# Moving the weight splits, the last pair's sums and copies, and small buffers in a fused attention and mixture-of-experts kernel

## The chip, the cores and the metric

One core of a Trainium2 chip runs the whole program. The metric is the time of one execution in device microseconds; "before" was run three times. TensorE is called PE in the profile, VectorE DVE, ScalarE ACT, GpSimd POOL and SyncE SP.

## The reference

Soft-capped attention of 4 batches, 12 heads, 448 positions and 64 channels; its output, 1792 tokens of 768 channels, goes through a mixture of 8 experts with one expert per token.

```python
scores = cap * tanh(q @ k.T / sqrt(64) / cap)
attn = softmax(scores)                       # exp, divided by the sum over keys
x = (attn @ v)                               # as [1792, 768]
logits = normalize(x) @ normalize(expert_emb).T / tau
e = argmax(logits); gate = softmax(logits)[e]
out[token] = gate * (relu(x[token] @ w1[e]) @ w2[e])     # w1: 768 x 1024, w2: 1024 x 768
```

## The kernel before

The attention works on pairs of heads, 24 in all, six to a batch. The loop of `attention_bounded` runs over i = 0 to 24, and in each i over four parts u = 0 to 3: PE makes part u of the scores of pair i and ACT turns them into probabilities (tanh at line 780, exp at line 784); at the same time PE multiplies the probabilities of the pair before, j = i - 1, with the values, part u (line 811, and line 820 in part 3). So i = 24 has only the values of pair 23. At part 2 DVE splits q and k of the next pair into a high and a low half (lines 756 and 757). After part 3, DVE copies the values of pair j out of PSUM (line 826; the PSUM tile "v" has one buffer), and `add_keys(i)` sums the seven tiles of probabilities over keys: first two and two on DVE (line 792), the rest on POOL (lines 794 and 800). For the last pair, where nothing comes after, half of the rest is on DVE (lines 798 and 800).

The order on each engine is the order in which the program is written down (a manual schedule). Four lists are worked off between the parts: `later` (what follows a pair: `norms` at line 837 sums over keys on PE and copies to `ds` at line 839; `rows` transposes the values on PE and scales them on DVE at line 866; `router` and more), `route` and `side` (the choice of experts for a batch), and `fill`.

`fill` holds the work on the first expert: once two batches have gone through, the expert with most tokens so far is taken first, and its weights are loaded in 14 pieces into a ring of three buffers. Each piece is split in two halves, 28 splits in all: ACT rounds a half to float16 (line 221) and DVE takes the rest (line 222), and after the second half SP loads the piece three further on (lines 691 and 694). One is taken from `fill` at a time, unless `hold` has entries, three after each of two steps of a batch's norms:

```python
if fill and u != 2 and not hold:
    fill.pop(0)()
```

Behind the loop, the first tile of the first expert begins: `transpose_x` (PE transposes at line 212, ACT and DVE copy at lines 215 and 216), then twelve steps `up(0, 0)` to `up(1, 5)` on PE (line 231), in each of which one entry of `later` and one of `fill` are taken, and a `relu` (lines 243 and 244) after each six. Then, in `tile0`, come the second half of the tile, and between its matmuls the choice of experts for the last batch. The branch that ends the attention (line 1122) leads to the second tile of the first expert. There DVE computes the order of the experts and the slots of all tokens (`order` and `slots`, lines 1174 to 1216), PE and DVE a table from it (lines 1227 and 1228), and POOL gathers the next tile's tokens with it. Tiles of the seven other experts follow, each expert's weights split while the tile before is computed.

Pools: `small` is open for the whole program; `apool` and `lpool` hold the attention's buffers; `work` is opened behind the attention and shares their memory.

Of the kernel before, what the change touches and what calls it, by code (L numbers as in the profile page):

```python
# [30 lines left out]
F32 = mybir.dt.float32  # L31
F32R = mybir.dt.float32r
F16 = mybir.dt.float16
I32 = mybir.dt.int32
AF = mybir.ActivationFunctionType
ALU = mybir.AluOpType
# [3 lines left out]
P = 128  # L40
B, H, S, DH = 4, 12, 448, 64
# [3 lines left out]
E = 8  # L45
# [3 lines left out]
G = 4 * B  # L49
# [31 lines left out]
def attention_moe(ctx: ExitStack, tc: tile.TileContext, q, k, v, cap, emb, tau, w1, w2, qk_pairs, v_pairs, out):  # L81
    nc = tc.nc
# [99 lines left out]
    sums = const.tile([P, NF], F32, name="sums")  # L182
# [85 lines left out]
    small = ctx.enter_context(tc.tile_pool(name="small", bufs=1))  # L268
    ps_t = ctx.enter_context(tc.tile_pool(name="ps_t", bufs=2, space=PSUM))
    with ExitStack() as actx:  # L270
# [71 lines left out]
        t = small.tile([P, 4, XW], F32, tag="xsb", name="xsb")  # L342
# [398 lines left out]
        def attention_bounded(apool, ps_s, ps_o):  # L741
# [18 lines left out]
            prob = {}  # L760
# [25 lines left out]
            psum_v = {}  # L786
            sums = {}

            def add_keys(i):
                pt = prob[i]  # L790
                t = apool.tile([P, 2, S], F32, tag="sums", name=f"sums{i}", bufs=3)
                nc.vector.tensor_tensor(t, pt[:, 0:2, :], pt[:, 2:4, :], op=ALU.add)  # L792
                if i < NPAIRS - 1:
                    nc.gpsimd.tensor_tensor(t, t, pt[:, 4:6, :], op=ALU.add)  # L794
                for s in range(2):
                    eng = nc.vector if i == NPAIRS - 1 and s == 0 else nc.gpsimd
                    if i == NPAIRS - 1:
                        eng.tensor_tensor(t[:, s, :], t[:, s, :], pt[:, 4 + s, :], op=ALU.add)
                    sl = slice(s * DH, (s + 1) * DH)
                    eng.tensor_tensor(t[sl, s, :], t[sl, s, :], pt[sl, 6, :], op=ALU.add)  # L800
                sums[i] = t

            def values(i, u):
                vb = loaded[i // 2][1][:, i % 2]
                pt = prob[i]
                if u == 0:
                    psum_v[i] = ps_o.tile([P, 512], F32, tag="v", name=f"v{i}")
                o = psum_v[i]
                if u < 3:
                    for s in range(2):  # L810
                        nc.tensor.matmul(  # L811
                            o[s * DH : (s + 1) * DH, :S],
                            vb[:, u, s * DH : (s + 1) * DH],
                            pt[:, 2 * u + s, :],
                            start=u == 0,
                            stop=False,
                            skip_group_check=True,
                        )
                else:
                    nc.tensor.matmul(  # L820
                        o[:, :S], vb[:, 3, :], pt[:, 6, :], start=False, stop=True, skip_group_check=True
                    )

                if u == 3:
                    x = apool.tile([P, S], F32, tag="xt", name=f"xt{i}", bufs=8)
                    nc.vector.tensor_copy(x, o[:, :S])  # L826
                    xt[i] = x

            xt = {}
# [2 lines left out]
            def norms(i):  # L832

                b, n = i // NP, i % NP
                d = ps_o.tile([P, 512], F32, tag="d", name=f"d{i}")
                for m in range(4):
                    nc.tensor.matmul(d[m * 32 : (m + 1) * 32, :S], ones32, sums[i + m // 2][:, m % 2, :], start=True, stop=True)
                ds = apool.tile([P, S], F32, tag="ds", name=f"ds{i}", bufs=1)
                nc.vector.tensor_copy(ds, d[:, :S])
                return ds  # L840

            def norms_t(i, ds):
# [59 lines left out]
            NPAIRS = B * NP  # L902
# [56 lines left out]
            with tc.manual_schedule():  # L959
                split_qk(0)  # L960
                for i in range(NPAIRS + 1):
                    j = i - 1
                    if i == 0:
                        route.extend(x for f in prepare for x in (f, lambda: None))
                    for u in range(4):
                        if i < NPAIRS:
                            scores(i, u)
                        if (i, u) == (0, 0):
                            split_qk(1)
                        if (i, u) == (0, 1):  # L970
                            warm_up()
                        if u == 2 and 0 < i < NPAIRS - 1:
                            split_qk(i + 1)
                        if j >= 0:
                            values(j, u)
                        if u != 2:
                            do_later()
                        if side:
                            side.pop(0)()
                        if u % 2 == 0 or i >= 3 * NP:  # L980
                            do_route()
                        if u == 1 and len(later) > 2:
                            do_later()
                        if fill and u != 2 and not hold:
                            fill.pop(0)()
                        if hold:
                            hold.pop()
                    if i % 2 == 0 and i // 2 + 2 < NH:
                        load_heads(i // 2 + 2)
                    if i < NPAIRS:  # L990
                        add_keys(i)
                    if j >= 0:
                        after(j)
                while route:
                    do_route()
                transpose_x(ps_t, "tt")
                scale_x()
                hp = [ps_s.tile([P, 2, 4, P], F32, tag="s", name=f"hp{h}")[:, 0] for h in range(2)]
                ups = [(h, j) for h in range(2) for j in range(DC)]
                while later or ups:  # L1000
                    do_later()
                    if ups:
                        h, j = ups.pop(0)
                        up(w1p[0], h, j, hp[h])
                        if j == DC - 1:
                            relu(h, hp[h], acc0, tiles=first_h[h])
                    if fill:
                        fill.pop(0)()
                yp = ps_s.tile([P, 2, 512], F32, tag="s", name="yp")
                tile0(fill, (lambda n, i: yp[:, i, :384] if n == "y" else x_tile, (ps_t, "tt")))  # L1010
# [133 lines left out]
    val = work.tile([P, NV, E], F32, tag="val", name="val")  # L1144
    by_pos = work.tile([P, NV, E], F32, tag="by_pos", name="by_pos")
    pos_i = work.tile([1, 2, E], I32, name="pos_i")
    pos_e = work.tile([1, E], I32, name="pos_e")
    perm = work.tile([P, E, E], F32, name="perm")
    table = work.tile([P, NTAB], I32, name="table")
    cp = {}  # L1150
    eid = {}
# [20 lines left out]
    def order():  # L1172

        nc.vector.tensor_tensor(
            perm,
            iota_t[:, :E].unsqueeze(2).to_broadcast([P, E, E]),
            place.unsqueeze(1).to_broadcast([P, E, E]),
            op=ALU.is_equal,
        )
        which = work.tile([1, E, E], F32, tag="which_e", name="which_e")  # L1180
        nc.vector.tensor_tensor(which, perm[0:1], iota_t[0:1, :E].unsqueeze(1).to_broadcast([1, E, E]), op=ALU.mult)
        with nc.allow_low_precision("numbers of experts, exact"):
            nc.vector.tensor_reduce(pos_e, which, axis=AX.X, op=ALU.add)

    def slots():
        every = work.tile([P, E], F32, tag="every", name="every")
        nc.vector.tensor_tensor(every, done_full, halves, op=ALU.add)
        gn = work.tile([P, E, E], F32, tag="gn", name="gn")
        nc.vector.tensor_tensor(gn, gt, every.unsqueeze(1).to_broadcast([P, E, E]), op=ALU.mult)
        first_t = work.tile([P, E], F32, tag="first_t", name="first_t")  # L1190
        nc.vector.tensor_reduce(first_t, gn, axis=AX.X, op=ALU.add)
        token_rows(last)

        both = work.tile([P, E], F32, tag="both", name="both")
        more = work.tile([P, E], F32, tag="more", name="more")
        nc.vector.scalar_tensor_tensor(out=both, in0=done_full, scalar=-31.0, in1=tails, op0=ALU.add, op1=ALU.mult)
        nc.vector.tensor_tensor(more, first_t, done_full, op=ALU.add)
        nc.vector.tensor_tensor(more, place, more, op=ALU.subtract)
        nc.vector.scalar_tensor_tensor(out=both, in0=both, scalar=32.0, in1=first_t, op0=ALU.mult, op1=ALU.add)
        nc.vector.scalar_tensor_tensor(out=more, in0=more, scalar=float(TAIL0), in1=tails, op0=ALU.add, op1=ALU.mult)  # L1200
        nc.vector.scalar_tensor_tensor(out=both, in0=more, scalar=1024.0, in1=both, op0=ALU.mult, op1=ALU.add)
        at = work.tile([P, G, E], F32, tag="at", name="at")
        nc.vector.tensor_tensor(at, oh_all, both.unsqueeze(1).to_broadcast([P, G, E]), op=ALU.mult)
        slot = work.tile([P, G], F32, tag="slot", name="slot")
        nc.vector.tensor_reduce(slot, at, axis=AX.X, op=ALU.add)
        packed, which, more = [work.tile([P, G], I32, tag=n, name=n) for n in ("packed", "which", "further")]
        nc.vector.tensor_scalar(packed, slot, 31.0 * 32, None, op0=ALU.add)
        nc.vector.tensor_scalar(which, packed, 5, 31, op0=ALU.logical_shift_right, op1=ALU.bitwise_and)
        nc.vector.tensor_scalar(more, packed, 10, None, op0=ALU.logical_shift_right)
# [453 lines left out]
```

## Time and profile before

| | us |
|---|---|
| runs | 547.07, 541.33, 545.64 |
| median | 545.64 |
| profiled execution | 543.0 |
| its span, first to last instruction | 541.3 |
| PE busy | 479.0 |
| DVE busy | 335.4 |
| ACT busy | 299.7 |
| POOL busy | 239.2 |

The profile is of one execution, with times from the start of its span. A row of the time line has the start, the duration, engine, line, operation, what it writes and reads, and in brackets how long the engine stood idle before it and what it stood for. Scores of pair 0 begin at 8 us, the values of pair 23 at 227 us, and the expert tiles take the rest.

### The profile page before, as it was taken

The page shows a single profiled execution, that of the slowest core. Times are in us where ns is not written, and L with a number is a line of the kernel's source. Part 1 is how long each engine was busy: PE and PEld are TensorE (multiplying, and loading weights), DVE is VectorE, ACT ScalarE, POOL GpSimd, SP SyncE. Part 2 cuts the span into 40 slices and gives each one's busy share as a digit, 9 for nine tenths or more (in the row PEclk, how much of TensorE's full clock was granted, in tenths as well). Part 3 has the DMA queues.
Part 4 walks back from the last instruction along what each step waited for, and adds up shares of the span by engine and source line. Part 5 has one row for each costly group of instructions (what it writes and reads, how often), then busy time and mean ns, then how long its engine had stood idle before and what let it go on. Part 6 is the DMA issues. An engine that isn't in the chain of part 4 may idle for free. (4 is left out here: it accounts for less than half of the span.)

```text
span 541.3 us, 11929 instructions
## 1 busy us (share of the span) xinstructions
PE 479.0 (88%) x4597; PEld 311.6 (58%) x4598; DVE 335.4 (62%) x713; ACT 299.7 (55%) x369; POOL 239.2 (44%) x289
## 2 busy tenths in 40 slices
PE   3999998999897988969879699999999999998970
PEld 1444443344433333337658488778887888787760
DVE  4877686968698899587738812591213921396811
ACT  3988788788877987917108301651114811386500
POOL 2567554655553355550125623562333643355321
PEclk9999999999999999979999799999999999999977
DMA  7433219321633540325189911293110952097940
GB/s 224 133 111 114 64 49 312 115 68 45 215 139 130 191 160 0 89 72 178 36 320 401 356 64 59 100 365 115 61 59 32 350 200 72 31 320 256 383 140 11
DMA packets 30514, 83.09 MB, mean 153 GB/s; under 512 B 7277, under 2 KB 7433, under 8 KB 30418
## 3 DMA queue, kind: packets, MB, share of 16 engines
q1 hardware_dynamic: 26354, 67.68, 35.9%
q0 software_dynamic: 2816, 12.61, 6.9%
q10 hardware_dynamic: 1248, 1.64, 0.9%
q8 instruction: 45, 0.74, 0.6%
q14 instruction: 51, 0.42, 0.2%
HBM read 69.51 MB, written 13.00 MB: 152 GB/s over the span
## 5 line engine op out<-in xcount | busy, mean ns | idle before, releaser
L780 ACT ACTIVATE prob<-s,icap 128x896 f32<-128x896 f32 x96 | 86.2, 903 | 25.8 <-PE s L774 18.2
L231 PEld LDWEIGHTS <-h 128*128 128x128 f16 x1056 | 81.5, 100 | 10.3 <-issue 6.6
L794 POOL TENSOR_TENSOR sums<-sums,prob 128x896 f32<-128x896 f32 x23 | 48.3, 2099 | 83.1 <-DVE sums L792 67.5
L784 ACT ACTIVATE prob<-prob,cap_b 128x896 f32<-128x896 f32 (+1 forms) x64 | 81.8, 1277 | 2.1
L231 PE MATMUL h<-xh,h 128*128 128x128 f16 (+1 forms) x480 | 79.6, 220 | 3.1 <-ACT x_tile L669 1.4
L231 PE MATMUL h<-xh,l 128*128 128x128 f16 (+1 forms) x480 | 79.6, 220 | 2.8 <-issue 2.8
L231 PE MATMUL h<-xl,h 128*128 128x128 f16 (+1 forms) x480 | 79.6, 220 | 0.0
L811 PE MATMUL v<-prob,vb 128*64 128x448 f32 x288 | 70.0, 565 | 3.0 <-DVE xt L826 2.9
L800 POOL TENSOR_TENSOR sums<-sums,prob 64x448 f32<-64x448 f32 x47 | 64.3, 1368 | 3.6
L204 POOL TENSOR_TENSOR x_tile<-xg 128x768 f32<-128x768 f32 x16 | 23.5, 1467 | 82.8 <-PE xt L212 72.9
L244 DVE SCALAR_TENSOR_TENSOR hl<-h,hh 128x512 f16<-128x512 f32 (+1 forms) x20 | 13.3, 664 | 65.3 <-ACT hh L243 65.3
L231 PEld LDWEIGHTS <-l 128*128 128x128 f16 x528 | 52.9, 100 | 0.8 <-issue 0.8
L243 ACT ACTIVATE hh<-h 128x512 f16<-128x512 f32 (+1 forms) x20 | 11.5, 574 | 70.1 <-PE h L231 70.1
L215 ACT CAST xh<-xt 128x384 f16<-128x384 f32 x30 | 13.1, 480 | 65.3 <-PE xt L212 57.3
L774 PE MATMUL s<-hi 64*128 64x448 f32 x144 | 34.8, 475 | 15.3 <-DVE hi L756 12.8
L1396 PE MATMUL h<-xh,h 128*128 128x160 f16 x192 | 39.9, 233 | 5.2 <-ACTq L1539 2.6
L638 PEld LDWEIGHTS <-hh 128*128 128x128 f16 (+1 forms) x352 | 32.9, 100 | 19.1 <-issue 0.5
L222 DVE SCALAR_TENSOR_TENSOR l<-w1r,by_pos,h 128x1024 f16<-128x1024 f32 x30 | 37.7, 1307 | 9.5 <-ACT h L221 9.5
L216 DVE TENSOR_TENSOR xl<-xt,xh 128x384 f16<-128x384 f32 x30 | 15.4, 551 | 43.6 <-ACT xh L215 43.5
L774 PEld LDWEIGHTS s<-hi 64*128 64x128 f32 x144 | 14.1, 188 | 47.7 <-ACT prob L780 18.9
L638 PE MATMUL y<-h,hl 128*128 128x384 f16 (+1 forms) x160 | 38.2, 329 | 2.0 <-DVE hl L244 2.0
L1396 PE MATMUL h<-xh,l 128*128 128x160 f16 x192 | 39.9, 233 | 0.0
(315 smaller groups left out, 1135.5 us busy)
## 6 DMA issues: line engine op xcount, KB each, us to landing
w1r<-in_moe_w_dram SPq DMA_DIRECT2D x36, 512.0 KB, 6.1
w2r<-in_moe_w_dram SPq DMA_DIRECT2D x24, 768.0 KB, 8.1
qkb<-in_qk_pairs_dram SPq DMA_DIRECT2D x11, 960.0 KB, 5.7
vb<-in_v_pairs_dram SPq DMA_DIRECT2D x12, 512.0 KB, 6.5
x_dram<-xsb SPq DMA_DIRECT2D x4, 1152.0 KB, 6.7
ring<-in_moe_w_dram SPq DMA_DIRECT2D x6, 512.0 KB, 4.0
ring<-in_moe_w_dram SPq DMA_DIRECT2D x8, 384.0 KB, 3.1
x_dram<-xsb ACTq DMA_DIRECT2D x1, 1152.0 KB
```

The costliest lines, as they stand in the source:

```text
L204: nc.gpsimd.tensor_tensor(x_tile, xg[:, :D], xg[:, SCALE : SCALE + 1].to_broadcast([P, D]), op=ALU.mult)
L216: nc.vector.tensor_tensor(lo, t, hi, op=ALU.subtract)
L222: nc.vector.scalar_tensor_tensor(out=lo, in0=raw, scalar=scale, in1=hi, op0=ALU.mult, op1=ALU.subtract, accum_out=acc)
L231: nc.tensor.matmul(hp[:, f, :W], l[j][:, c], x[:, j, :W], start=j == 0 and f == 0 and n == 0, stop=j == DC - 1 and f == 3 and n == 2, skip ...
L638: nc.tensor.matmul(y, hidden[h][l][:, c, o : o + k], w2p[p % 2][w][f // 2][:, f % 2, m * C : (m + 1) * C], start=f == 0 and n == 0, stop=f ...
L774: nc.tensor.matmul(sp[:, s, :S], l[sl, kc], r[sl, :], start=n == 0, stop=n == 2)
L780: nc.scalar.activation(o, d, AF.Tanh, scale=icap)
L784: nc.scalar.activation(o, o, AF.Exp, scale=cap_b)
L794: nc.gpsimd.tensor_tensor(t, t, pt[:, 4:6, :], op=ALU.add)
L800: eng.tensor_tensor(t[sl, s, :], t[sl, s, :], pt[sl, 6, :], op=ALU.add)
L811: nc.tensor.matmul(o[s * DH : (s + 1) * DH, :S], vb[:, u, s * DH : (s + 1) * DH], pt[:, 2 * u + s, :], start=u == 0, stop=False, skip_grou ...
L1396: nc.tensor.matmul(o, w1p[p % 2][l][j][:, c], x[:, j, :], start=j == 0 and f == fs[0] and m == 0, stop=j == DC - 1 and f == fs[-1] and m == 2,
```

## The change

- `fill` is taken from at all four parts of a pair, and no longer while i = 24.
- The first add of the last pair's sums (two tiles and two on DVE) has its own function, `add_two`, and is written at part 2 of i = 23, behind that part's split, instead of after part 3.
- The copy of the last pair's values and of the last sums over keys (`ds` of pairs 22 and 23) go from DVE to ACT.
- The small tiles of `order` and `slots` are taken from `small` instead of `work`.

```diff
+            def add_two(i):
+                pt = prob[i]
+                t = sums[i] = apool.tile([P, 2, S], F32, tag="sums", name=f"sums{i}", bufs=3)
+                nc.vector.tensor_tensor(t, pt[:, 0:2, :], pt[:, 2:4, :], op=ALU.add)
+
             def add_keys(i):
-                pt = prob[i]
-                t = apool.tile([P, 2, S], F32, tag="sums", name=f"sums{i}", bufs=3)
-                nc.vector.tensor_tensor(t, pt[:, 0:2, :], pt[:, 2:4, :], op=ALU.add)
+                if i < NPAIRS - 1:
+                    add_two(i)
+                pt, t = prob[i], sums[i]
...
-                sums[i] = t
...
-                    nc.vector.tensor_copy(x, o[:, :S])
+                    (nc.vector.tensor_copy if i < NPAIRS - 1 else nc.scalar.copy)(x, o[:, :S])
...
-                nc.vector.tensor_copy(ds, d[:, :S])
+                (nc.vector.tensor_copy if i < NPAIRS - 2 else nc.scalar.copy)(ds, d[:, :S])
...
-                        if fill and u != 2 and not hold:
+                        if fill and not hold and i < NPAIRS:
                             fill.pop(0)()
                         if hold:
                             hold.pop()
+                        if (i, u) == (NPAIRS - 1, 2):
+                            add_two(i)
...
-    pos_e = work.tile([1, E], I32, name="pos_e")
-    perm = work.tile([P, E, E], F32, name="perm")
+    pos_e = small.tile([1, E], I32, name="pos_e")
+    perm = small.tile([P, E, E], F32, name="perm")
...
-        every = work.tile([P, E], F32, tag="every", name="every")
+        every = small.tile([P, E], F32, tag="every", name="every")
...
```

The lines left out at the end do the same for `which_e`, `gn`, `first_t`, `both`, `more`, `at`, `slot`, `packed`, `which` and `further`.

## Rows read from the trace of the kernel before

**Rows 1.** The page of the kernel before, its parts 1 and 2.

```profile
PE 479.0 (88%) x4597; PEld 311.6 (58%) x4598; DVE 335.4 (62%) x713; ACT 299.7 (55%) x369; POOL 239.2 (44%) x289
...
PEclk9999999999999999979999799999999999999977
```

**Rows 2.** Busy time by stretch: PE, PEld, DVE, ACT, POOL, granted clock, DMA.

```profile
190.00:195.00 5.00, 4.11 (x23) 2.12 (x21) 4.90 (x11) 4.93 (x6) 4.04 (x3) 1.00 0.13 23
...
236.00:238.00 2.00, 1.21 (x7) 0.55 (x11) 2.00 (x6) 0.87 (x3) 0.42 (x2) 0.74 0.00 0
...
240.00:242.00 2.00, 2.00 (x16) 1.89 (x16) 1.48 (x4) 0.00 (x0) 0.00 (x0) 0.50 0.00 0
...
243.50:244.00 0.50, 0.50 (x4) 0.08 (x4) 0.00 (x0) 0.00 (x0) 0.00 (x0) 0.70 0.92 369
...
516.00:518.00 2.00, 0.00 (x0) 0.00 (x0) 0.00 (x0) 0.00 (x0) 0.00 (x0) 0.72 0.47 163
```

**Rows 3.** Time line of PE: start, duration, line, idle time before.

```profile
218.09 0.97 PE L811 MATMUL v<-prob,vb 128*64 128x448 f32 x4
...
227.40 0.97 PE L811 MATMUL v<-prob,vb 128*64 128x448 f32 x4 [0.28 <-DVE xt L826]
...
235.38 0.52 PE L212 MATMUL xt<-ident,x_tile 128*128 128x128 f32 x3 [3.08 <-DVE xsb L866]
...
240.00 0.27 PE L231 MATMUL hp<-xl,h 128*128 128x128 f16 x1 [0.62 <-DVE xl L216]
```

**Rows 4.** Time line of DVE at the end of the attention.

```profile
219.51 0.75 DVE L222 SCALAR_TENSOR_TENSOR l<-ring,first_s,h 128x512 f16<-128x512 f32 x1 [1.47 <-ACT h L221]
...
220.19 1.09 DVE L792 TENSOR_TENSOR sums<-prob 128x896 f32<-128x896 f32 x1
...
229.62 2.01 DVE L792 TENSOR_TENSOR sums<-prob 128x896 f32<-128x896 f32 x1
...
233.13 1.43 DVE L800 TENSOR_TENSOR sums<-sums,prob 64x448 f32<-64x448 f32 x1
...
237.64 1.83 DVE L222 SCALAR_TENSOR_TENSOR l<-ring,first_s,h 128x384 f16<-128x384 f32 x1
```

**Rows 5.** The two lines of a split: minimum/median/maximum ns.

```profile
L221 ACT ACTIVATE h<-ring,first_s x28: 597/616/718, 165.0 to 252.7; 128x384 f16<-128x384 f32 x16, 128x512 f16<-128x512 f32 x12
L222 DVE SCALAR_TENSOR_TENSOR l<-ring,first_s,h x28: 583/733/1992, 165.8 to 253.4; 128x384 f16<-128x384 f32 x16, 128x512 f16<-128x512 f32 x12
```

**Rows 6.** Time line of ACT in pairs 18 to 23.

```profile
170.09 0.23 ACT L428 ACTIVATE ex<-lg 128x32 f32<-128x32 f32 x1 [2.40 <-DVE lg L427]
...
187.30 1.01 ACT L780 ACTIVATE prob<-s,icap 128x896 f32<-128x896 f32 x1 [0.51 <-issue]
...
217.54 0.62 ACT L780 ACTIVATE prob<-s,icap 128x448 f32<-128x448 f32 x1
...
226.84 0.61 ACT L780 ACTIVATE prob<-s,icap 128x448 f32<-128x448 f32 x1
...
235.94 0.48 ACT L215 CAST xh<-xt 128x384 f16<-128x384 f32 x1 [5.76 <-PE xt L212]
```

**Rows 7.** Time line of POOL, sums of pairs 22 and 23.

```profile
227.16 2.10 POOL L794 TENSOR_TENSOR sums<-sums,prob 128x896 f32<-128x896 f32 x1
...
234.16 1.39 POOL L800 TENSOR_TENSOR sums<-sums,prob 64x448 f32<-64x448 f32 x1
```

**Rows 8.** Time line of PE behind the splits.

```profile
256.56 0.18 PE L443 MATMUL rp<-oh_all,upper 128*128 128x32 f16 x1 [0.92 <-DVE oh_all L422]
...
272.20 0.56 PE L1227 MATMUL tabp<-bm,a_all 128*128 128x40 f16 x16 [2.81 <-DVE bm L1216]
```

**Rows 9.** Time line of DVE behind the splits.

```profile
253.93 0.69 DVE L244 SCALAR_TENSOR_TENSOR hl<-hp,hh 128x512 f16<-128x512 f32 x1
...
265.58 0.22 DVE L1174 TENSOR_TENSOR perm<-iota_t,place 128x64 f32<-128x64 f32 x1 [2.36 <-issue]
```

**Rows 10.** The branch of DVE at line 1122.

```profile
L1122 DVEq COMPARE_BRANCH  x2: 50/52/53, 6.2 to 262.6; - x2
```

More of the change, by code (lines that the diff above doesn't have):

```diff
@@ L1179, in order @@
         )
-        which = work.tile([1, E, E], F32, tag="which_e", name="which_e")
+        which = small.tile([1, E, E], F32, tag="which_e", name="which_e")
         nc.vector.tensor_tensor(which, perm[0:1], iota_t[0:1, :E].unsqueeze(1).to_broadcast([1, E, E]), op=ALU.mult)
@@ L1185, in slots @@
     def slots():
-        every = work.tile([P, E], F32, tag="every", name="every")
+        every = small.tile([P, E], F32, tag="every", name="every")
         nc.vector.tensor_tensor(every, done_full, halves, op=ALU.add)
-        gn = work.tile([P, E, E], F32, tag="gn", name="gn")
+        gn = small.tile([P, E, E], F32, tag="gn", name="gn")
         nc.vector.tensor_tensor(gn, gt, every.unsqueeze(1).to_broadcast([P, E, E]), op=ALU.mult)
-        first_t = work.tile([P, E], F32, tag="first_t", name="first_t")
+        first_t = small.tile([P, E], F32, tag="first_t", name="first_t")
         nc.vector.tensor_reduce(first_t, gn, axis=AX.X, op=ALU.add)
         token_rows(last)
-        both = work.tile([P, E], F32, tag="both", name="both")
-        more = work.tile([P, E], F32, tag="more", name="more")
+        both = small.tile([P, E], F32, tag="both", name="both")
+        more = small.tile([P, E], F32, tag="more", name="more")
         nc.vector.scalar_tensor_tensor(out=both, in0=done_full, scalar=-31.0, in1=tails, op0=ALU.add, op1=ALU.mult)
@@ L1201, in slots @@
         nc.vector.scalar_tensor_tensor(out=both, in0=more, scalar=1024.0, in1=both, op0=ALU.mult, op1=ALU.add)
-        at = work.tile([P, G, E], F32, tag="at", name="at")
+        at = small.tile([P, G, E], F32, tag="at", name="at")
         nc.vector.tensor_tensor(at, oh_all, both.unsqueeze(1).to_broadcast([P, G, E]), op=ALU.mult)
-        slot = work.tile([P, G], F32, tag="slot", name="slot")
+        slot = small.tile([P, G], F32, tag="slot", name="slot")
         nc.vector.tensor_reduce(slot, at, axis=AX.X, op=ALU.add)
-        packed, which, more = [work.tile([P, G], I32, tag=n, name=n) for n in ("packed", "which", "further")]
+        packed, which, more = [small.tile([P, G], I32, tag=n, name=n) for n in ("packed", "which", "further")]
         nc.vector.tensor_scalar(packed, slot, 31.0 * 32, None, op0=ALU.add)
```

## The prediction

> **What bounds the kernel now.** I read the page first, for the share of each engine and for the clock by slice [rows 1]: TensorE (PE) is busy 88% of the span, and its granted clock falls in four of the 40 slices; one of them, slice 18, holds the end of the attention, which the change edits. Then the busy time by stretch [rows 2]: the clock falls to 0.50 at about 237 and is on its way back in the last half microsecond before 244, although PE has work from 239 on. The time line of PE says why [rows 3]: the last values of pair 23 begin at 227.40; then PE stands for 3.08 us until 235.38, for DVE's line 866, and after some first work again for 0.62 until 240.00, for DVE's line 216. The time line of DVE [rows 4] shows what those wait behind: from 229.62 the last pair's three sums (2.01 us, then twice 1.43, of which one row stands), later a split of 1.83 us at 237.64. So the end of the attention is bound by DVE's order, and its stall costs twice: the idle time, and half a clock afterwards.
>
> After 240 the work is one chain (first tile, choice, table, gather, second tile), whose waits on PE all name DVE or what DVE feeds; a shift at 240 goes through to the end at full size, as the expert tiles follow in program order.
>
> **The splits.** From the program, one split (ScalarE, then DVE) is popped per part. Before, a pair has splits at parts 0, 1, 3, and 24 has three beside the values; after, parts 0 to 3 of pairs up to 23. Counting the list of 28 through the loop, and the parts that are held back, 14 come out before the end of pair 23 now and 20 in the changed kernel: one more at the third part of each of pairs 17, 18, 19, 20, 22, 23. Three leave the values of the last pair and three the tile's first half (11 to 8). The total stays at 28. One costs ACT 0.6 us and DVE 0.7 [rows 5].
> Pairs 17 to 20: ACT stands 2.40 us before 170.09 and then not at all until 0.51 before 187.30 [rows 6], so pair 17's extra split lies mostly in idle time (DVE is behind it: 0.3 of 0.7 shows), and those of 18 and 19 cost ACT their full 0.6 each. On DVE the one of 19 comes after the next pair's q and k and pushes what follows by about 1.7 in all; from 184.6 to 217.9 DVE is busy all but a few hundredths (4.90 of 5 us in the stretch of [rows 2]), so pair 20's 0.7 adds in full. Sum at 217.9: **+2.4 us**. Bounds: 0 (the extra work falls into ACT's and PE's gaps and onto better moments between GpSimd's operations) and 4 x 0.7 = 2.8.
> Pair 22: the third part's split on ACT can begin when the exponential ends, at 217.54 [rows 6], so DVE, which then idles 1.47 until 219.51 [rows 4], waits until 218.2 and does the split until 218.9; only then comes the copy of the last values out of the PSUM tile "v", which has one buffer. Counted without the 2.4, the copy ends at 219.5 where PE wanted the tile at 218.09 [rows 3]: PE is pushed by 1.4. The index of the first gather is behind the same split, so GpSimd's chain moves by 1.5 and its last sum ends at 236.9, not 235.55 [rows 7]; the sum over keys on PE wants it at about 237.6, so this is covered by 0.7 us.
>
> **The last sums.** The add of pair 23's first four tiles moves ahead of the copy of pair 22's values. It is queued on DVE behind the split of the third part, which waits for ACT: that pair's exponential ends at 226.84 [rows 6]; with PE's 1.4 and the split it is 228.3. Split until 228.95, add until 230.95 with the 2.01 of [rows 4], copy until 231.5. The copy is waited for by PE's values of pair 23: they begin at 231.5 where they began at 227.40, after 3.0 us of idle PE. So the stall doesn't vanish, it moves ahead of the values. The add would be 1.09 alone, as it is for pair 22 [rows 4]; that end would give 2.1 us of stall. Both ends stay; I take 2.01, because GpSimd's 2.10 us sum of pair 22 [rows 7] begins at 228.7 by the same shift.
> The Trainium skill (SBUF — State Buffer, "SBUF: two separate sides") says that the port pair of DVE and GpSimd is an exclusive lock held for a whole instruction. The slow rows of DVE agree with a hold-up beside GpSimd's sums; by the rule in full the add would be 1.09 + 2.10 = 3.2 us and the stall 4.2.
> After the copy DVE has one split and the two sums left (1.43 each), to 235.65, and the two rows of line 866 end at 236.3 and 237.0. PE's values and transposes take 4.9 us from 231.5, so PE comes to the tile's transposes at 236.4 and is hardly held. With no split behind them, and with the copy of pair 23's values and of its sums on idle ACT (0.6 each, hidden: ACT stands 5.76 us there [rows 6]), the first matmul with both operands is at 238.6 instead of 240.00: **-1.4 us**.
>
> **The clock.** At 0.50 from 240.0 to 243.8, PE does what takes half as long at full clock: 1.9 us. If the 3.0 us stall ahead of the values doesn't drop the clock, **-1.9 us**. The rows speak for both: a gap of 2.81 before 272.20 [rows 8] left it full; in the 2 us without any PE work from 516 to 518 it fell (0.72 on average, [rows 2]).
>
> **Behind the splits.** With three fewer, ACT and DVE are done with splits four steps before the first half of the tile is. Now DVE's line 244 starts at 253.93 because of them [rows 9], and PE stands 0.92 until 256.56 for the choice that follows it [rows 8]. I count **-0.7 us**, the split time ahead of line 244; 0 if the choice meets another wait.
>
> **The buffers.** The small tiles of the order and the slots move to a pool that doesn't share memory with the attention. DVE stands 2.36 us before the first of them at 265.58 [rows 9], but the row names no releaser, and the branch out of the attention was issued at 262.6 [rows 10]: I read it as the branch, which stays. **0**; bounds 0 and -2.4.
>
> **Sum**: 2.4 - 1.4 - 1.9 - 0.7 = -1.6 us against the profiled execution's 543.0 (span 541.3 and 1.7 around it), 541.4. The median of the runs, 545.64, is 2.6 above that execution; on its scale the forecast is **544.0**.
>
> **Rivals.**
> (1) Slower: the clock falls in the new stall, ahead of the values. It is decided by whether the stall of PE before the values is long enough; the row of 516 to 518 speaks for it, the one at 272.20 against. Then the 4.9 us of values run at half clock until about 238.3 (the slow stretch lasts 6.8 us now), the tile starts at 242.0 in place of 240.0, and is at full clock from there: 2.4 + 2.0 - 1.9 - 0.7 = +1.8, so 547.4. The lock rule of the Trainium skill (SBUF — State Buffer, "SBUF: two separate sides") would lead here. Worked from rows, GpSimd's 2.10 in full ahead of the add makes the stall 4.2 us and the time 548.6; the slow rows so far show 2.01 for such an add, so I give this 0.07 of the rival's chance.
> (2) The scores absorb the extra splits: PE and ACT have idle time in pairs 18 to 21, and DVE's operations there are anything from 0.6 to 2.0 us long by where GpSimd stands [rows 5]. Then the 2.4 goes: -4.0, so 541.6. Against it: DVE next to never idle for 33 us.
> (3) The wait before 265.58 is for the attention's memory after all, and the buffers take it away: -1.6 - 2.4 = -4.0, also 541.6. Against it: no releaser named.
> (4) The edit does not do what it says: the stall only changes its place and the clock its phase, the sums cancel: 545.6.
>
> **How the numbers follow.** Forecast 0.43, rival (1) 0.25, (2) 0.17, (3) 0.05, (4) 0.10. The range goes from 541.6 less 2 (the runs shown differ by 5.7 among themselves, a median of them by less) to 547.4 plus 1: 539.5 to 548.5. About 1%, 5.4 us, is what a measurement of this kernel can tell from no change; none of the cases reaches it alone. Over 1% faster needs (2), (3) and the clock together, 0.11; over 1% slower needs (1) with the lock rule's price and a loop that pays 4 us, 0.09; within 1% 0.80.
>
> **What would show it.** In the changed profile: the scores of pair 23 begin about 2.5 to 3 us later; PE stands 2 to 3 us before the values of pair 23, and no longer 3 us before line 212; the clock is full in the stretch in which the first tile starts; line 244's second run starts right after ACT's; the idle time before the first order instruction stays near 2.4 us. Wrong would be: a clock of 0.5 over the values, a loop that ends as early as now, or a pool wait that vanishes.

## The result and the profile after

The changed kernel takes 547.55 us (median), beside 544.5 us for the kernel before, run on the same chips: ratio 1.0056, 95% interval 1.0037 to 1.0075, so 3.0 us slower where 1.6 us faster was forecast. Ratios leave out the executions that lie over 1.5% above the fastest of their kernel; the profiled execution of h1 (below) is one of those. The profiled execution of the changed kernel has a span of 544.9 us (541.3 before). The first lines are its page, to be read beside [rows 1]: the clock of slice 18 is 8, not 7, but slices 15, 17, 21 and 37 are below 9 now too.

```profile
PE 482.6 (89%) x4597; PEld 313.3 (58%) x4598; DVE 332.6 (61%) x711; ACT 300.9 (55%) x371; POOL 241.4 (44%) x289
...
PEclk9999999999999989889989799999999999998987
```

The time line of PE after (lines below the edit are 4 to 6 higher than before: 811 is 815, 826 is 830, 866 is 870):

```profile
222.50 1.30 PE L815 MATMUL v<-prob,vb 128*64 128x448 f32 x4 [1.89 <-DVE xt L830]
...
236.90 1.76 PE L815 MATMUL v<-prob,vb 128*64 128x448 f32 x4 [4.09 <-DVE xt L830]
...
242.22 1.02 PE L824 MATMUL v<-prob,vb 128*128 128x448 f32 x2
243.08 0.82 PE L212 MATMUL xt<-ident,x_tile 128*128 128x128 f32 x6
...
244.84 0.22 PE L231 MATMUL hp<-xl,h 128*128 128x128 f16 x1
```

Against [rows 3], the wait of 3.08 us ahead of line 212 and that of 0.62 ahead of line 231 are gone, as forecast; in their place PE stands 4.09 us ahead of the values of pair 23 and 1.89 us ahead of the first values beside that pair, each time for the copy of line 830. What the second copy stands behind is on the time line of DVE (against [rows 4]):

```profile
232.75 1.62 DVE L222 SCALAR_TENSOR_TENSOR l<-ring,first_s,h 128x384 f16<-128x384 f32 x1 [1.85 <-ACT h L221]
...
234.31 2.00 DVE L792 TENSOR_TENSOR sums<-prob 128x896 f32<-128x896 f32 x1
236.23 0.61 DVE L830 COPY xt<-v 128x448 f32<-128x448 f32 x1
...
237.70 1.54 DVE L803 TENSOR_TENSOR sums<-sums,prob 128x448 f32<-128x448 f32 x1
239.27 1.43 DVE L805 TENSOR_TENSOR sums<-sums,prob 64x448 f32<-64x448 f32 x1
240.63 1.55 DVE L870 TENSOR_TENSOR xsb<-xb,inv 128x384 f32<-128x384 f32 x4
```

DVE does nothing for 1.85 us because ACT's half of the third part's split lies behind that part's exponential; then come split, early add and copy, 4.1 us, in which PE has nothing to do. ACT's half of the split and its copy of the last values, and POOL's sums:

```profile
232.12 0.60 ACT L221 ACTIVATE h<-ring,first_s 128x384 f16<-128x384 f32 x1
...
243.28 0.53 ACT L830 COPY xt<-v 128x448 f32<-128x448 f32 x1 [8.84 <-PE v L824]
```

```profile
231.87 2.08 POOL L799 TENSOR_TENSOR sums<-sums,prob 128x896 f32<-128x896 f32 x1
234.03 3.27 POOL L805 TENSOR_TENSOR sums<-sums,prob 64x448 f32<-64x448 f32 x2
```

By stretch (columns as in [rows 2]) the clock is 1.00 while PE stands, then falls to 0.50 over the values that follow the stall, and is back before the tile starts:

```profile
234.00:236.00 2.00, 0.00 (x0) 0.00 (x0) 2.00 (x3) 0.44 (x1) 1.90 (x2) 1.00 0.14 59
236.00:238.00 2.00, 1.10 (x4) 0.29 (x4) 2.00 (x7) 0.00 (x0) 1.92 (x2) 0.67 0.00 0
238.00:240.00 2.00, 2.00 (x8) 0.96 (x8) 1.97 (x2) 0.00 (x0) 1.92 (x2) 0.50 0.56 192
240.00:242.00 2.00, 2.00 (x12) 0.59 (x8) 1.94 (x5) 0.00 (x0) 0.68 (x2) 0.98 0.02 9
```

Behind the splits, DVE's rows answer to [rows 9]: line 244 waits for ACT's half alone, and the order still stands for its branch.

```profile
256.56 0.69 DVE L244 SCALAR_TENSOR_TENSOR hl<-hp,hh 128x512 f16<-128x512 f32 x1 [1.35 <-ACT hh L243]
...
268.11 0.23 DVE L1180 TENSOR_TENSOR perm<-iota_t,place 128x64 f32<-128x64 f32 x1 [2.26 <-issue]
```

The same marks in five traces, one execution each, the kernel before in us of its span (differences taken before rounding), the others as their distance from it (the columns right of "after" are experiments, below; a kernel's column begins with what its own execution won or lost ahead of the edit):

| starts | before | after | g1 | g2 | g4 |
|---|---|---|---|---|---|
| tanh of pair 18 | 165.63 | -0.08 | -1.96 | +0.15 | -1.09 |
| tanh of pair 22 | 208.55 | +2.35 | +0.75 | +4.80 | +1.87 |
| tanh of pair 23 | 219.38 | +3.50 | +1.16 | +5.10 | +3.72 |
| values of pair 23 | 227.40 | +9.50 | +1.03 | +5.00 | +9.79 |
| second matmul of the tile | 240.00 | +4.83 | -1.39 | +2.79 | +3.88 |
| first order instruction of DVE | 265.58 | +2.54 | -3.32 | +1.80 | +1.73 |
| end | 541.30 | +3.63 | -0.46 | +2.28 | +3.02 |

### The profile page after: what moved, and what is told of

Same layout as the page of the kernel before. It is cut to its first block, busy times and chain, and to the rows that moved or that the text cites. A ratio compares the mean times of both kernels' runs of the same rounds, so it can differ in the third digit from the quotient of the medians.

```text
span 544.9 us, 11932 instructions
## 1 busy us (share of the span) xinstructions
PE 482.6 (89%) x4597; PEld 313.3 (58%) x4598; DVE 332.6 (61%) x711; ACT 300.9 (55%) x371; POOL 241.4 (44%) x289
## 5 line engine op out<-in xcount | busy, mean ns | idle before, releaser
L231 PEld LDWEIGHTS <-h 128*128 128x128 f16 x1056 | 80.4, 100 | 5.4 <-issue 1.7
L815 PE MATMUL v<-prob,vb 128*64 128x448 f32 x288 | 72.9, 586 | 10.2 <-DVE xt L830 10.2
L1402 PE MATMUL h<-xh,h 128*128 128x160 f16 x192 | 41.0, 237 | 4.8 <-ACTq L1545 2.6
L216 DVE TENSOR_TENSOR xl<-xt,xh 128x384 f16<-128x384 f32 x30 | 15.4, 552 | 46.6 <-ACT xh L215 46.5
L1402 PE MATMUL h<-xh,l 128*128 128x160 f16 x192 | 41.0, 237 | 0.0
L1402 PE MATMUL h<-xl,h 128*128 128x160 f16 x192 | 41.0, 237 | 0.0
```

What stands on the lines that cost most here:

```text
L216: nc.vector.tensor_tensor(lo, t, hi, op=ALU.subtract)
L231: nc.tensor.matmul(hp[:, f, :W], l[j][:, c], x[:, j, :W], start=j == 0 and f == 0 and n == 0, stop=j == DC - 1 and f == 3 and n == 2, skip ...
L815: nc.tensor.matmul(o[s * DH : (s + 1) * DH, :S], vb[:, u, s * DH : (s + 1) * DH], pt[:, 2 * u + s, :], start=u == 0, stop=False, skip_grou ...
L1402: nc.tensor.matmul(o, w1p[p % 2][l][j][:, c], x[:, j, :], start=j == 0 and f == fs[0] and m == 0, stop=j == DC - 1 and f == fs[-1] and m == 2,
```

## The experiments

**Which part costs.** Each part alone, and all but one. Ratios are to the kernel before on the same chip.

The split rule alone (e1), the early add alone (e2):

```diff
-                        if fill and u != 2 and not hold:
+                        if fill and not hold and i < NPAIRS:
```

> The kernel before with the change to the splits alone (all four parts, none while i = 24). Theory A, the splits in the third part cost the loop 3.5 us (work on ACT and DVE that was not idle, and waits of DVE for ACT ahead of the copy out of "v"), and the place of the add only shifts work inside DVE's order: +3 us against the kernel before, scores of pair 23 begin 3.5 us later, values of pair 23 about 7.5 us later. Theory B, the add's new place is what costs (its 2.0 us sit ahead of the copy): +1 us, as the splits are given back behind the loop.

```diff
+            def add_two(i):
...
+                        if (i, u) == (NPAIRS - 1, 2):
+                            add_two(i)
```

> The kernel before with the add of the last pair's first tiles at part 3 of pair 23 and nothing else. Theory A: DVE stands idle there when no split waits, so the values of pair 23 begin at most 0.5 us later, and the 2.0 us leave the order ahead of line 866: PE's 3.08 us wait shrinks to about 1, -2 us, up to -3.5 if the clock then stays full. Theory B: the add delays the copy out of "v" by its own 1 to 2 us: 0 to +1 us.

e1 measured 1.0044 (1.0018 to 1.0071), 2.4 us slower; e2 0.9972 (0.9952 to 0.9992), 1.5 us faster, the lowest ratio of all versions here. The copies and buffers together (e3), apart (e5, e6), and the buffers a second time (f2, the same program as e6):

```diff
-                    nc.vector.tensor_copy(x, o[:, :S])
+                    (nc.vector.tensor_copy if i < NPAIRS - 1 else nc.scalar.copy)(x, o[:, :S])
...
-    perm = work.tile([P, E, E], F32, name="perm")
+    perm = small.tile([P, E, E], F32, name="perm")
```

> The kernel before with the two copies on ACT and the small tiles in the other pool. Both theories: the copies take 0.6 us from DVE ahead of line 216 and ACT is idle there, -0.5 us, not below -1; the buffers 0 (idle time of 2.3 us before the first order instruction stays). If the buffers free a wait: -2.5 us and that idle time goes.

> The kernel before with the two copies on ACT alone. The run with copies and buffers together was 2.3 us slower in the median, though its profile is 1.9 us ahead of the kernel before when the order of the experts begins. Theory A, the copies gain and the buffers cost: -1 to -2 us. Theory B, the copies cost (ACT is late for what follows them): +2 us.

> The kernel before with the small tiles in the other pool alone. Theory A, the addresses or the code behind the attention cost: +2.5 to +4 us, all of it behind the first expert. Theory B: 0. Theory C, the difference of the last run is between executions and not of the edit: 0 here and 0 for the copies.

> The buffers alone once more. Theories A and B: +2 us again, above 0.2% with its interval. Theory C: between -0.15 and +0.15%.

e3 1.0042 (1.0016 to 1.0067), e5 1.0002 (0.9980 to 1.0025), e6 1.0036 (1.0011 to 1.0060), f2 1.0030 (1.0008 to 1.0052). So the copies cost nothing that can be measured and the buffers 0.3%, twice, where I had 0. The trace of f2 shows no place for it (its wait before the first order instruction is 2.50 us, 2.36 before). To see whether any shift of addresses does the same, f1 moved another tile of `work` into `small`:

```diff
-        pv = work.tile([P, NV, E, E], F32, tag="pv", name="pv")
+        pv = small.tile([P, NV, E, E], F32, tag="pv", name="pv")
```

> The kernel before with one other tile, the products of the positions (1280 bytes a partition, near the 1312 of the change's small tiles), taken from the small pool, and the change's tiles left where they were. Theory A, the move of all later buffers by some 1.3 KB costs: +2 us, as the change's buffers did. Theory B, what costs is that the order's own tiles lie elsewhere: 0. Theory C, the buffers' 2 us came from the phase of the clock in those executions: 0.

1.0018 (0.9992 to 1.0043): between the two answers. All but one part: without the early add (e4: parts as in e1 and e3), without the buffers (f4), and early add with copies (f3).

> The changed kernel with the add back in its old place. Theory A: within 1 us of the changed kernel, so +2 to +3.5 us against before: the stall ahead of the values of pair 23 shrinks from 4.1 to about 2.1 us, the one ahead of line 212 comes back by as much. Theory B: the 2.0 us of the add come back in full: +0.5 to +1 us against before.

> The changed kernel with the small tiles back in their old pool. If the parts add up (splits +2.4, add -1.5, copies 0.1): +1 us against before. If the buffers cost nothing: +3 us, as the changed kernel.

> The kernel before with the early add and the two copies on ACT, the splits and the buffers as before. The copies gave 0 alone; with the add out of the way, DVE has line 216 earlier still: -1.5 to -2.5 us. If copies and add save the same wait: -1 to -1.5 us, as the add alone.

e4 1.0084 (1.0052 to 1.0116), f4 1.0093 (1.0063 to 1.0123), f3 0.9997 (0.9968 to 1.0025). With f4 the buffers' price isn't found again: without them the kernel should be faster than the changed one, and isn't. The split rule is in all versions so far that are slower than e3; e3 and e6 are slow by the buffers. What it does to the stall is seen in PE's rows ahead of the values of pair 23, first of e1, then of f4:

```profile
234.62 0.97 PE L811 MATMUL v<-prob,vb 128*64 128x448 f32 x4 [2.20 <-DVE xt L826]
```

```profile
236.10 1.76 PE L815 MATMUL v<-prob,vb 128*64 128x448 f32 x4 [4.67 <-DVE xt L830]
```

The split alone makes 2.20 us of stall, and the early add, which queues behind it, lengthens it to over 4.

**Which half of the split rule.** e7 takes splits at all four parts and goes on in the last values; e8 takes none in the last values and none at the third part.

```diff
-                        if fill and u != 2 and not hold:
+                        if fill and not hold:
```

> The kernel before with splits at all four parts, and still beside the last values. If the third part's splits are what costs (3.5 us until pair 23, of which the work taken out of the tail gives back little): +3 us, at most 1 us from the run with the whole change of the splits. If dropping the splits beside the last values is what gains there: +4 to +5 us.

```diff
-                        if fill and u != 2 and not hold:
+                        if fill and u != 2 and not hold and i < NPAIRS:
```

> The kernel before with no splits while i = 24, and the third part left out as before. The three splits leave DVE's order ahead of lines 866 and 216 (0.7, 0.6 and 1.8 us) and come three steps later in the tile's first half, where DVE has room: -1.5 to -2.5 us. If the choice behind the first half waits for the splits instead: 0 to -0.5, with the run of line 244 that much later.

e7 1.0091 (1.0059 to 1.0123). e8 1.0085 (1.0055 to 1.0115), a miss. Its ACT and PE rows tell why: 14 splits are out when the tile begins, not 17 as in the kernel before, so two are left for the tile's second half; the load of the last weights, which follows the splits of earlier pieces, comes so late that ACT stands for it, and the choice of experts, behind that split on DVE, keeps PE waiting 6.74 us.

```profile
253.84 0.61 ACT L221 ACTIVATE h<-ring,first_s 128x384 f16<-128x384 f32 x1 [5.68 <-DMA ring<-in_moe_w_dram]
```

```profile
258.19 0.19 PE L443 MATMUL rp<-oh_all,upper 128*128 128x32 f16 x1 [6.74 <-DVE oh_all L422]
```

So the two halves of the rule belong together: whoever takes the splits out of the last values needs others earlier. That leaves the question which of the third-part splits hurt.

**Which splits, and through what.** g1 is the changed kernel without the third-part splits of pairs 22 and 23; g2 keeps them and the early add but writes both behind the copy; g3 is the kernel before with early add and splits as in g1, copies and buffers as before; g4 puts 14 matmuls whose result nothing uses into the stall.

```diff
-                        if fill and not hold and i < NPAIRS:
+                        if fill and not hold and i < NPAIRS and (u != 2 or i < NPAIRS - 2):
```

> The changed kernel, but at the third part of pairs 22 and 23 no split is taken (two more are left for the tile's first half). Measured before it: the changed kernel at 1.0056 of the kernel before, the early add alone at 0.9972, the splits alone at 1.0044. If the price lies in the stall ahead of the values of pair 23 (4.09 us in the changed kernel's profile), the stall shrinks to 1.5 to 2.5 us (the early add is still ahead of the copy) and the time falls by 1.4 to 3 us, to 0 to +1.5 us against the kernel before. If the price lies in the extra splits of pairs 17 to 20, the time stays within 1 us of the changed kernel's, at +2 to +4 us.

g2 has that line too, and below it

```diff
+                        if fill and not hold and u == 3 and NPAIRS - 2 <= i < NPAIRS:
+                            fill.pop(0)()
...
-                        if (i, u) == (NPAIRS - 1, 2):
+                        if (i, u) == (NPAIRS - 1, 3):
```

> The changed kernel with the same number of splits, but those of the third part of pairs 22 and 23, and the early add, are written behind the copy of the values out of the tile v. If what counts is where PE stands (ahead of the values), values of pair 23 begin some 4 us earlier, and the time falls by about 3 us, to 0 against the kernel before. If what counts is the sum of DVE's work ahead of its last two products, the stall only moves back to the place that it had in the kernel before (ahead of the sums over keys), and the time stays within 1 us of the changed kernel's.

> The kernel before with the early add and with the splits at the third part of pairs 17 to 20 alone (none in pairs 22 and 23, none in the last values); copies and buffers as before. If the loop's extra splits are nearly free and the stall is what costs: the early add's -1.5 us and about -0.5 for the tile, so -1 to -2 us against the kernel before. If the loop's splits cost their counted 2.4 us or more: 0 to +1.5 us.

```diff
+            def keep_busy(n):
+                d = ps_o.tile([P, 512], F32, tag="d", name="busy")
+                for _ in range(n):
+                    nc.tensor.matmul(d, ones16, a_all[:, 0:4, :], start=True, stop=True)
...
+                        if (i, u) == (NPAIRS, 0):
+                            keep_busy(14)
```

> The changed kernel with 14 matmuls of 512 columns more, whose result nothing uses, on TensorE ahead of the values of pair 23 (about 3 us, inside the stall of 4.09 us; they add no work that must be done). If the clock's fall in that stall is part of the price, the clock stays at 1.00 over the values (0.50 to 0.67 in the changed kernel from 236 to 240) and the time falls by 1.5 to 2 us against the changed kernel, to about +1 us against the kernel before. If the fall is hidden (DVE's last products end when they end, whatever PE's clock was), the time is within 0.7 us of the changed kernel's.

g1 measured 0.9994 (0.9972 to 1.0015): 0.62% or 3.4 us less than the changed kernel, and the intervals don't touch. The two splits that g1 leaves for the tile carry the whole loss by this comparison. Its PE and DVE rows:

```profile
228.43 0.97 PE L815 MATMUL v<-prob,vb 128*64 128x448 f32 x4 [0.28 <-DVE xt L830]
...
235.45 1.42 PE L212 MATMUL xt<-ident,x_tile 128*128 128x128 f32 x6 [2.12 <-DVE xsb L870]
```

```profile
226.05 0.69 DVE L222 SCALAR_TENSOR_TENSOR l<-ring,first_s,h 128x384 f16<-128x384 f32 x1 [2.10 <-ACT h L221]
226.68 0.08 DVE L222 DVE_READ_ACCUMULATOR l<-ring,first_s,h 128x1 f32 x1
226.68 1.08 DVE L792 TENSOR_TENSOR sums<-prob 128x896 f32<-128x896 f32 x1
227.75 0.62 DVE L830 COPY xt<-v 128x448 f32<-128x448 f32 x1
```

The early add is still ahead of the copy, but it runs in time that DVE had idle and at its own 1.08 us, before POOL's sum begins; the copy is as early as in the kernel before (wait 0.28, as in [rows 3]). So the add costs nothing at this place by itself; it lengthens the stall (2.20 us in e1, 4.09 with it) only when the split stands ahead of it, and without the add (e4) the kernel is no faster.

g2 measured 1.0022 (0.9994 to 1.0050), 0.34% below the changed kernel, with intervals that overlap. PE has no stall ahead of the values but one ahead of line 212 again, of 3.30 us (3.08 in [rows 3]):

```profile
232.40 0.97 PE L815 MATMUL v<-prob,vb 128*64 128x448 f32 x4 [0.28 <-DVE xt L830]
...
240.60 1.18 PE L212 MATMUL xt<-ident,x_tile 128*128 128x128 f32 x6 [3.30 <-DVE xsb L870]
```

In the table g2's tile starts 2.0 us earlier than the changed kernel's although its pair 23 began 1.6 us later. DVE's work ahead of line 870 does count (the stall comes back), but where it stands counts too.

g3 measured 0.9977 (0.9954 to 1.0000), as fast as e2 within the intervals: the extra splits of pairs 17 to 20 and the ones kept out of the last values cancel to nothing that can be measured.

g4 measured 1.0041 (1.0016 to 1.0066), 0.8 us below the changed kernel, not told apart by time. Its stretches show that the clock stays full over the values:

```profile
234.00:236.00 2.00, 2.00 (x10) 0.72 (x8) 2.00 (x3) 0.71 (x2) 1.85 (x3) 1.00 0.29 120
236.00:238.00 2.00, 0.86 (x5) 0.20 (x4) 2.00 (x7) 0.00 (x0) 1.92 (x2) 1.00 0.00 0
238.00:240.00 2.00, 2.00 (x14) 0.97 (x12) 1.97 (x4) 0.00 (x0) 1.92 (x2) 1.00 0.42 115
```

and its tile starts 0.95 us earlier than the changed kernel's, though its values of pair 23 begin 0.29 later (table): from the values to the tile's transposes PE takes 4.73 us, not 6.18.

```profile
237.19 0.97 PE L821 MATMUL v<-prob,vb 128*64 128x448 f32 x4 [1.14 <-DVE xt L836]
...
241.92 1.07 PE L212 MATMUL xt<-ident,x_tile 128*128 128x128 f32 x6
```

The fall in the stall is thus worth about 1 us at the tile, a third of the 3.0, less than the 1.5 to 2 expected; this is one trace, and the stall beside pair 22 is as it was.

**Pair 22 or pair 23.** h1 leaves out pair 23's third-part split alone, h2 pair 22's.

```diff
-                        if fill and not hold and i < NPAIRS:
+                        if fill and not hold and i < NPAIRS and (i, u) != (NPAIRS - 1, 2):
```

> The changed kernel without the split at the third part of pair 23 alone. If that split is what holds the early add and the copy, the stall of 4.09 us ahead of the values of pair 23 all but goes, and the time falls by 2 to 3 us, to 0 to +1 us against the kernel before. If pair 22's split is the costly one, the time stays within 1 us of the changed kernel's (+3 us).

```diff
-                        if fill and not hold and i < NPAIRS:
+                        if fill and not hold and i < NPAIRS and (i, u) != (NPAIRS - 2, 2):
```

> The changed kernel without the split at the third part of pair 22 alone. By the sum of the trace it takes 1.9 us of stall and up to 1 us of slow clock out of pair 22, but the 4 us stall of pair 23 stays: 0.5 to 1.5 us less than the changed kernel, +1.5 to +2.5 us against the kernel before. If pair 22's push were hidden behind the stall of pair 23: no difference from the changed kernel.

h1 1.0023 (0.9995 to 1.0052), h2 1.0110 (1.0077 to 1.0143). PE's wait ahead of the values of pair 23 in the two profiled executions, h1 first:

```profile
222.53 0.97 PE L815 MATMUL v<-prob,vb 128*64 128x448 f32 x4 [1.23 <-DVE xt L830]
...
232.27 0.97 PE L815 MATMUL v<-prob,vb 128*64 128x448 f32 x4 [1.00 <-DVE xt L830]
```

```profile
237.33 1.76 PE L815 MATMUL v<-prob,vb 128*64 128x448 f32 x4 [5.18 <-DVE xt L830]
```

Without pair 23's split the stall is 1.00 us, without pair 22's 5.18, and without either 0.28. By time, leaving out pair 23's saves 0.33% with pair 22's kept (intervals overlap) and 1.16% without it (they don't). Pair 22's alone gives no consistent sign: leaving it out costs 0.54% beside pair 23's, and saves 0.29% without it. I expected h2 to be 0.5 to 1.5 us faster than the changed kernel and it is 2.9 slower; in its trace pair 21 begins 5.65 us later than in the kernel before, measured from pair 18, ahead of anything that this edit touches, so part of it is not the edit's: from the first scores of pair 18 to those of pair 22, eleven executions with the new rule in these pairs took 44.6 to 48.6 us, and h2's is the longest of them. Why it is slower by time stays open.

## Why the prediction was wrong

**Bound and place**: right. The end of the attention is bound by DVE's order, and the change moved the stall to the values of pair 23, as the step on the last sums says.

**The sum, term by term**: in the trace the loop is +3.5 at the first scores of pair 23 (2.4 counted), from there to the tile's second matmul +1.3 (-1.4 counted), from there to the order -2.3 (-2.6 counted), and behind the order +1.1, where nothing was counted. That makes 3.6.

**The splits of pairs 17 to 20**: about right. +2.4 counted, +2.35 at the first scores of pair 22, behind all of them. That this one pair of traces agrees is partly luck, as the clock stayed full in the loop of the kernel before and not in that of the changed one (last section); but from pair 18 to pair 22 the nine executions with the old rule there took 44.1 us in the mean (42.9 to 47.1), the eleven with the new one 46.6, so about 2.5 more. By time, however, together with the splits kept out of the last values they cost nothing net: g3 against e2 is 0.9977 against 0.9972. The other 1.1 us of the +3.5 arise in pair 22: ACT waits there for line 427 of DVE, which took 1.17 us in the changed kernel, where a POOL sum began at 215.36, and 0.19 before, and pair 22's own third-part split takes ACT's 0.5.

```profile
213.24 0.19 DVE L427 TENSOR_TENSOR lg<-lg,den 128x32 f32<-128x32 f32 x1
```

```profile
215.37 1.17 DVE L427 TENSOR_TENSOR lg<-lg,den 128x32 f32<-128x32 f32 x1
```

**The last sums: the step that failed.** It counted a stall of 3.0 us in place of 3.08, and a tile 1.4 us earlier for it. The stall measured 4.09. Where the values of pair 23 begin, counted 231.5 + 2.4 = 233.9, measured 236.90, the 3.0 us come apart in the rows: 0.7 from the loop (pair 22's third exponential ends at 220.65, 3.1 later than before, not 2.4); 0.7 from there to pair 23's third exponential, which ends at 232.12 (PE stood 1.89 beside pair 22, not 1.4, and the clock then fell there too, which I had not counted); 0.6 because ACT's half of the split (0.60 at 232.12) lies ahead of DVE's, and I let DVE begin at the exponential's end; 0.9 because DVE's half took 1.62, not 0.65, beside POOL's sum. The add took 2.00 as counted. The slow clock beside pair 22, in PE's row behind the 1.89 and by stretch:

```profile
223.73 1.72 PE L841 MATMUL d<-sums,ones 128*32 128x448 f32 x8
```

```profile
224.00:226.00 2.00, 2.00 (x12) 0.57 (x6) 1.03 (x2) 1.44 (x2) 1.77 (x1) 0.50 0.58 187
```

From the values of pair 23 to the tile's second matmul it took 7.94 us, not the 7.1 counted (231.5 to 238.6), since the clock fell over the values: 0.8. So this matmul came at 244.84, 3.8 later than 238.6 + 2.4 = 241.0.
The deeper mistake was to call the stall only moved. In the kernel before, PE stands 3.08 us for sums that have to be made; in the changed one DVE first waits 1.85 us for ACT, with the early add, the copy and PE's values queued behind. g1, where the add is in the same place and PE waits 0.28, shows that the stall comes from the split ahead of it, and that without these two splits the gain forecast for the tile is there: from the first scores of pair 23 to the tile's second matmul g1 needs 2.55 us less than the kernel before (1.16 to -1.39 in the table), where the changed kernel needs 1.33 more. By time g1 is still only as fast as the kernel before (0.9994).

**The clock and the choice**: about right. From the tile's second matmul to the order, the changed kernel needs 2.3 us less (4.83 to 2.54 in the table), where 1.9 + 0.7 = 2.6 was counted. How much of it is the edit's is not shown: e5, with the copies alone, needs 1.6 less in its one trace.

**"A shift at 240 goes through to the end at full size"**: not so in single executions. The changed kernel lost 1.1 us behind the order, g1 2.9 (-3.32 to -0.46 in the table). At the place that spoke for a full clock in the prediction, the gap ahead of line 1227 (1233 after; 2.81 in [rows 8]), the changed kernel's clock fell:

```profile
274.74 0.69 PE L1233 MATMUL tabp<-bm,a_all 128*128 128x40 f16 x16 [2.70 <-DVE bm L1222]
```

```profile
274.00:276.00 2.00, 1.26 (x24) 1.26 (x24) 1.79 (x8) 0.00 (x0) 0.21 (x1) 0.55 0.59 180
```

**The buffers**: 0 counted with bounds 0 and -2.4; alone they cost 0.3% twice. That lies outside the bounds. f1 and f4 leave the cause, and whether it acts inside the full change, open.

**Rival (1)** came nearest: the clock fell in the new stall, and its 547.4 is what was measured. But by g4 the fall is about 1 of the 3 us; the agreement is in part luck. The stall of 4.2 us by the lock rule of the Trainium skill (SBUF — State Buffer, "SBUF: two separate sides") is near the measured 4.09, by another sum: the add was 2.00, not 3.2. The hold-up fell on the split, which took 1.62 in place of 0.6 and ended at 234.37, 0.42 after a POOL sum that had begun before it. Rivals (2) and (3) are out: the traces of the loop show about 2.5 more with the new rule, and the wait before the order is 2.26.

## What to carry to other kernels

Before a piece of work is slipped in front of a copy on an in-order engine, ask what that piece itself waits for: here a filler of 0.6 us waited 1.85 us for another engine, and everything queued behind it, a useful early add too, became part of a stall that only the filler made. Four more fillers (pairs 17 to 20), with three fewer beside the last values, cost nothing that can be measured by time (g3), and two (pairs 22 and 23) cost the whole change, so fillers are stopped where the queue behind them has a consumer with nothing else to do. The version to keep is the one part that measured faster by itself: the early add of e2, 0.28% below the kernel before. That is one measurement; with the copies beside it (f3) the gain was not found again.

## What the runs showed of the hardware that was not expected

The length of one and the same DVE instruction depends on where POOL stands, by more than the rows of before show (0.58 to 1.99 us in [rows 5]): the split that takes 0.62 us alone took 2.27 in h2, where a POOL sum of 2.08 began 0.23 ahead of it.

```profile
232.54 2.27 DVE L222 SCALAR_TENSOR_TENSOR l<-ring,first_s,h 128x384 f16<-128x384 f32 x1 [1.77 <-ACT h L221]
```

```profile
232.31 2.08 POOL L799 TENSOR_TENSOR sums<-sums,prob 128x896 f32<-128x896 f32 x1
```

A single profile is a thin base for what the clock does in a loop: that of the kernel before has no fall to 0.50 between 172 and 213 us, but of the eight others whose program is the same up to pair 22, all but e3 have one or two (e6 at 173 and at 197). I had read the loop's times from the one execution without them. The gap ahead of the table's matmuls (line 1227 in the kernel before) is as thin a base: it is 2.6 to 3.4 us long in 19 of the 20 profiled executions, and the clock fell to 0.50 in it or just behind it in 14 of them and stayed full in five, one of which is the kernel before.
